# The feed-forward's transposed input: 32x32 blocks moved one by one, or through a scratch in DRAM

## The chip, the cores and the metric

The kernel runs on one core of one Trainium2 chip. Its engines are TensorE (PE, matrix products), VectorE (DVE), ScalarE (ACT), GpSimd (POOL) and SyncE (SP); SP here only issues DMA transfers, and all DMA transfers of this kernel are issued by SP, one after the other. The metric is the device time of one execution in microseconds (us). The kernel before takes 1178.18 us, the median of three runs from 1177.28 to 1179.29 us.

## The reference, cut to what matters

One transformer block on 2048 rows of 448 numbers, in float32: layer norm, attention with 16 query heads and one shared key and value head, a residual sum, then a second layer norm and a gated feed-forward with 1792 hidden features, and a second residual sum.

```python
x = A_x                                   # 1 x 2048 x 448
h = x + _A_ref(_layernorm(x), wq, wk, wv, wo)      # attention, head width 28
h2 = h + _B_ref(_layernorm(h), w1, w3, w2)

def _B_ref(x, w1, w3, w2):                # 448 -> 1792 -> 448
    gate = jnp.einsum("bsd,df->bsf", x, w1)
    up = jnp.einsum("bsd,df->bsf", x, w3)
    h = _silu(gate) * up
    return jnp.einsum("bsf,fd->bsd", h, w2)
```

The change concerns `_layernorm(h)`, the input of the feed-forward, on its way from rows to columns.

## The kernel before, in words

**Quarters and blocks.** The 2048 rows are worked in four quarters of 512 rows (`t` from 0 to 3, `T = 512`), and a quarter in four blocks of 128 rows (`n` from 0 to 3). The residual stream of a quarter stays in SBUF as `X[t]`, with rows on partitions. The matrix products need the normalized rows turned round, with the 448 features on partitions: the tile `xh`, which holds the features in three chunks of 128 partitions and a fourth of 64, and 512 columns, one for each row of the quarter.

**Order of the work.** The order on every engine is written out by hand. After a short start (projections of the queries, keys and values), the attention runs over 256 steps (16 per group of four heads, four groups a quarter), and between them hangs work from a table: `at(s, fn, ...)` puts a call at step `s`. The feed-forward follows: 14 steps `k` a quarter (`NF = 14`, 128 hidden features each), with a second table: `on(t, k, fn, ...)` puts a call behind step `k` of quarter `t`, and `k + 0.5` is a place a little later in the same step. In each step PE makes the two products of 128 hidden features (`ffn1_half`, two halves of the array working side by side, line 1025) and, for the step before, the product back to 448 (`ffn2_half`, line 1025 too). Between the halves stands `settle`, a 1x1 ACT copy out of the PSUM bank (line 1029): PE goes on to the other half only after it.

**The path of the feed-forward's input.** For each block, `ln_norm` (line 213) writes the normalized rows into a tile `xn`; `blocks` (line 225) transposes it on DVE in blocks of 32x32, so that inside every 32x32 block features and rows have changed places, while the blocks themselves still stand where they stood. Sixteen DMA transfers a block (`moves`, line 238), so 64 a quarter, then bring these small blocks to their places in `xh`, from SBUF to SBUF. Each takes 32 partitions of `xn`, and three or four pieces of 32 numbers (128 bytes) of each. `move(m)` issues the next `m` of the waiting transfers. Last, `split_x` (line 243 on ACT, 247 on DVE) divides `xh` chunk by chunk into a rounded part and a rest, the two operands of the products.

**When.** The input of quarter 0 is made during the attention (transposes behind groups of quarters 1 and 2, and two moves at each of 16 steps). The input of quarter `t` from 1 to 3 is made during the feed-forward of quarter `t - 1`: transposes behind steps 1, 3, 5 and 7, with all 16 moves at once, and `split_x` behind steps 9 to 12 (at `9.5 + n`). Quarter 1 differs: its transposes stand behind steps 1, 3, 4 and 6, the moves of its first two blocks follow at once, and the other 32 are spread, seven at each of the steps 4 to 8. In that quarter SP also has the last weights of the feed-forward to load, between the moves: `load_w13` (lines 175 to 177, six transfers a step) and `load_w2` (line 184), into buffers which the attention has left.

**Queues.** SP works its transfers off in program order, and a transfer whose data is not ready holds all that stand behind it. The transfers take eight semaphores in turn, and a transfer waits until the one eight places ahead of it has landed where it takes over that semaphore. ACT, DVE and PE work off their orders in the same way.

Of the kernel before, what the change touches and what calls it, by code (L numbers as in the profile page):

```python
# [8 lines left out]
F32 = mybir.dt.float32  # L9
# [7 lines left out]
P = 128  # L17
S = 2048
D = 448
# [3 lines left out]
T = 512  # L23
NT = S // T
NQ = T // P
# [10 lines left out]
def block_kernel(  # L36
# [13 lines left out]
    ve, se, ge, pe, sy = nc.vector, nc.scalar, nc.gpsimd, nc.tensor, nc.sync  # L50
# [4 lines left out]
    def f(ap):  # L55
        return ap.bitcast(F32)
# [6 lines left out]
    dr_pool = ctx.enter_context(tc.tile_pool(name="dr", bufs=2, space=DRAM))  # L63
# [152 lines left out]
    XT = {}  # L216

    def xt_tiles():
        return [xt_pool.tile([P, m, T], F32R, name=name) for m, name in ((4, "xh"), (3, "xl"))]

    XD, moves = {}, []

    def blocks(t, n):
        xt = ln_pool.tile([P, 512], F32, name="xn", bufs=4)
        ve.transpose(xt[:, :D], LN[t][3][n][:, :D])
        if n == 0:
            XT[t] = xt_tiles()
        to = f(XT[t][0])
        x4 = xt.rearrange("i (c b j) -> i c b j", c=4, b=4)
        for a in range(4):  # L230
            for b in range(4):
                m = 4 if b < 2 else 3
                moves.append((to[32 * b : 32 * b + 32, :m, n * P + 32 * a : n * P + 32 * a + 32],
                              x4[32 * a : 32 * a + 32, :m, b]))

    def move(m):
        for _ in range(min(m, len(moves))):
            sy.dma_start(*moves.pop(0))  # L238

    def split_x(t, *cs, high=None):  # L240
        raw, hi = XT[t][:2]
# [589 lines left out]
    def at(s, fn, *args):  # L831
        todo.setdefault(s, []).append((fn, args))
# [6 lines left out]
    for i in range(NI - 1):  # L839
        e = NC * (i + 1)  # L840
# [3 lines left out]
    for t in range(NT - 1):  # L844
        e = NC * NG * (t + 1)


        if t == 1:
            at(e + 14.7, ln_stats, 0, NQ - 1)
            at(e + 14.7, ln_rstd, 0)  # L850
        for n in range(NQ):
            at(e + 14.7, wo_rows, t, n)
            for m in {(1, 1): (0,), (1, 2): (1,), (2, 0): (2, 3)}.get((t, n), ()):
                at(e + 14.7, ln_norm, 0, m, True)
                at(e + 14.7, blocks, 0, m)
            if t == 0 and n == NQ - 1:
                continue
            late = NC * NG * (t + 2) + 14 if t < 2 else LAST - 12
            at(e + 14.7 if n < NQ - 1 else late + 0.7, ln_stats, t, n)
        if t:  # L860
            at(late + 2, ln_rstd, t)
            for k in range(16):
                at(e + 16 + k, move, 2)
    for c in range(4):
        at(LAST - 12 + 2 * c, lambda c: split_x(0, c, high=ve.tensor_copy), c)
    for t in range(NT - 1):
# [12 lines left out]
    for s in range(AHEAD, LAST):  # L879
        i, c = divmod(s, NC)  # L880
        n, kt = divmod(c, NQ)
# [221 lines left out]
    def on(t, k, fn, *args):  # L1103
        after.setdefault((t, k), []).append((fn, args))
# [20 lines left out]
    on(0, 12, ln_rstd, tl)  # L1125
    for t in range(1, NT):
        for n in range(NQ):
            k = (1, 3, 4, 6)[n] if t == 1 else 1 + 2 * n
            on(t - 1, k, ln_norm, t, n)
            on(t - 1, k, blocks, t, n)  # L1130
            if t > 1 or n < 2:
                on(t - 1, k, move, 16)
            on(t - 1, 9.5 + n, split_x, t, n)
    for k in range(4, 9):
        on(0, k, move, 7)

    prev = None
    for t in range(NT):
# [68 lines left out]
```

## Time and profile before

| what | value |
|---|---|
| median of three runs | 1178.18 us |
| the profiled execution | 1178.61 us |
| its span, first to last instruction | 1176.8 us |
| PE busy | 1150.6 us, 98% of the span |
| DVE busy | 806.6 us, 69% |
| ACT busy | 764.3 us, 65% |
| POOL busy | 328.9 us, 28% |
| mean granted clock of PE | 0.993 of full speed |
| attention ends, feed-forward begins | at about 739 us |

A row of the timeline gives the start, the duration, the engine, the line, the operation, what it writes and reads and, in square brackets, how long the engine stood idle before it and what ended that. A row with a count (x16) holds that many instructions, and its duration runs from the first one's start to the last one's end. SPq is SP's issuing of transfers; the duration is that of the issue, and the transfer itself lands later. A row of the windows view gives a stretch of the span, its length, and for PE, PE's weight loads, DVE, ACT and POOL the busy time in it with the number of instructions; then the granted clock, the share of the 16 DMA engines that was busy, and GB/s.

### The profile page before, as it was taken

To read this page: it belongs to the slowest core of one execution; us is meant where nothing else is said; L and a number is where in the kernel's file an instruction comes from. 1 tells how busy PE (TensorE), PEld (TensorE's weight loads), DVE (VectorE), ACT (ScalarE), POOL (GpSimd) and SP (SyncE) were. 2 spreads that over 40 slices of the span, in tenths; PEclk is the share of its full clock that TensorE was granted. 3 is DMA by queue.
4 is the path that set the end of the run, shared out by engine and by line. 5 is a ranking of instruction groups with operands and counts; after the bars stand their busy time and mean duration, and the time that the engine had idled before them with its cause. 6 is when DMAs were issued, how large, how long until landed. Compare 5 with 4: busy or idle time off the path is not lost.

```text
span 1176.8 us, 25851 instructions
## 1 busy us (share of the span) xinstructions
PE 1150.6 (98%) x10154; PEld 772.5 (66%) x10154; DVE 806.6 (69%) x1498; ACT 764.3 (65%) x1587; POOL 328.9 (28%) x242
## 2 busy tenths in 40 slices
PE   8999999999999999999999999999499999999998
PEld 6664444446444445444455443799499999999997
DVE  8878999997999988989988962544253454344333
ACT  5649999996999997999997999312122222222221
POOL 5312001111110111110111013334265555556552
PEclk9999999999999999999999999999799999999999
DMA  4010100001000001100011100223201101100000
GB/s 165 10 37 1 43 12 9 19 22 39 19 19 7 14 24 40 32 20 15 7 40 36 20 18 19 64 68 95 58 33 17 18 1 40 17 9 32 1 2 32
DMA packets 67834, 34.51 MB, mean 29 GB/s; under 512 B 44672, under 2 KB 62336, under 8 KB 67712
## 3 DMA queue, kind: packets, MB, share of 16 engines
q1 hardware_dynamic: 67712, 32.86, 10.6%
q8 instruction: 80, 1.31, 0.5%
q14 instruction: 42, 0.34, 0.1%
HBM read 20.37 MB, written 3.80 MB: 21 GB/s over the span
## 4 chain that ended last, share of the span: by engine, by line
PE 85%; SPq 7%; DVE 2%; ACT 2%; DMA 1%; issue 1%; POOL 0%; ACTq 0%; DVEq 0%; POOLq 0%
PE po L424 20%; PE pb L408 19%; PE pa L1025 16%; PE pa L324 10%; PE pb L1025 8%; PE pb L166 4%; SPq L238 4%; PE po L1025 4%; PE pa L166 3%; SPq L177 1%; SPq L175 1%; ACT OT L431 1%; SPq L176 1%; ACT ab L345 1%; DVE mx L334 1%
## 5 line engine op out<-in xcount | busy, mean ns | idle before, releaser
L334 DVE TENSOR_REDUCE mx<-pa 128x1 f32<-128x512 f32 x689 | 440.2, 685 | 22.2 <-PE pb L408 13.1
L408 PE MATMUL pb<-qs,KS 32*128 32x512 f32 x3072 | 384.8, 425 | 0.0
L415 ACT ACTIVATE pt<-pb 128x512 f32<-128x512 f32 x684 | 366.1, 621 | 20.0 <-PE pb L408 17.3
L408 PEld LDWEIGHTS pb<-qs,KS 32*128 32x128 f32 x3072 | 233.9, 182 | 132.8 <-ACT pt L415 66.9
L324 PE MATMUL pa<-KS,qs 32*128 32x512 f32 x886 | 311.6, 459 | 1.5 <-ACT ab L345 0.2
L1025 PE MATMUL pa<-xl,qs 64*128 64x512 f32 x1044 | 193.6, 389 | 0.0
L324 PEld LDWEIGHTS pa<-KS,qs 32*128 32x128 f32 x886 | 138.6, 182 | 83.2 <-DVE mx L334 46.4
L424 PE MATMUL po<-pt,VA 128*32 128x512 f32 x1368 | 182.2, 604 | 0.4 <-ACT pt L415 0.4
L1025 PE MATMUL pa<-xh,qs 64*128 64x512 f32 x739 | 157.6, 389 | 0.0
L455 POOL TENSOR_TENSOR OT<-OT,rb 128x512 f32<-128x512 f32 x15 | 19.5, 1300 | 458.2 <-DMA rb<-sd 206.9
L1025 PE MATMUL pb<-w2s,pt 64*128 64x448 f32 x1050 | 143.2, 360 | 0.0
L1025 PEld LDWEIGHTS pa<-xl,qs 64*128 64x128 f32 x1044 | 140.2, 185 | 3.2
L1035 DVE TENSOR_TENSOR pt<-pa,pt 128x512 f32<-128x512 f32 x49 | 33.9, 691 | 152.7 <-ACT pt L1033 146.6
L1025 PEld LDWEIGHTS pb<-w2s,pt 64*128 64x128 f32 x1050 | 123.1, 184 | 2.4 <-DVE pt L1041 0.4
L352 DVE CUSTOM_DVE_ANT_0 ab<-pa,ab 128x512 f32<-128x512 f32 x138 | 93.6, 686 | 39.0 <-PE pa L324 27.1
L1025 PEld LDWEIGHTS pa<-xh,qs 64*128 64x128 f32 x739 | 106.7, 185 | 3.1
L415 ACT ACTIVATE xl<-pb 128x512 f32<-128x512 f32 x170 | 99.7, 611 | 9.0 <-PE pb L408 6.8
L415 ACT ACTIVATE xh<-pb 128x512 f32<-128x512 f32 x170 | 104.5, 633 | 0.0
L1033 ACT ACTIVATE pt<-pa 128x512 f32<-128x512 f32 x49 | 29.3, 597 | 96.9 <-PE pa L1025 92.8
L424 PE MATMUL po<-xl,VA 128*32 128x512 f32 x340 | 89.4, 605 | 0.0
L424 PE MATMUL po<-xh,VA 128*32 128x512 f32 x340 | 89.4, 605 | 0.0
L345 ACT ACTIVATE ab<-pa 128x512 f32<-128x512 f32 x138 | 82.2, 608 | 6.5 <-PE pa L324 4.9
(156 smaller groups left out, 1412.9 us busy)
## 6 DMA issues: line engine op xcount, KB each, us to landing
rb<-sd SPq DMA_DIRECT2D x64, 64.0 KB
QR<-OT SPq DMA_DIRECT2D x60, 56.0 KB
QR<-in_B_w_dram SPq DMA_DIRECT2D x16, 192.0 KB
X<-in_A_x_dram SPq DMA_DIRECT2D x3, 896.0 KB
out_dram<-X SPq DMA_DIRECT2D x3, 896.0 KB
xh<-xn SPq DMA_DIRECT2D x128, 16.0 KB
xh<-xn SPq DMA_DIRECT2D x128, 12.0 KB
w<-in_B_w_dram SPq DMA_DIRECT2D x8, 192.0 KB
```

Source lines behind the costliest of these rows:

```text
L166: pe.matmul(ps, lhs[b][:, cb, lsl], (rhs[2] if ca == 3 and len(rhs) == 3 else rhs[a])[:, ca, rsl], start=(k == 0), stop=(k == len(terms) - 1),
L238: sy.dma_start(*moves.pop(0))
L324: pe.matmul(ps, QS[i][r, 0, n * P : (n + 1) * P], KS[0][r, kt * T : (kt + 1) * T] if keys is None else keys[r], start=True, stop=True)
L334: ve.tensor_reduce(self.to(), ps, axis=AX.X, op=ALU.max)
L345: se.activation(self.ab, ps, AF.Relu)
L352: ve.tensor_tensor_reduce(self.ab, ps, self.ab, 1.0, -3.0e38, ALU.add, ALU.max, self.to())
L408: pe.matmul(self.ps, KS[k % 2][r, c * P : (c + 1) * P], QS[i][r, k // 2], start=(k == 0), stop=(k == 2))
L415: se.activation(f(PT[i, c, p][:, jj]), self.ps, AF.Exp, bias=0.0, scale=SCALE)
L424: pe.matmul(PO[i][32 * j : 32 * j + 32], VA[:, c], f(PT[i, c, j // 2][:, j % 2]), start=(c == 0), stop=(c == NC - 1))
L1025: pe.matmul(ps[:, : rhs.shape[-1]], lhs, rhs, start=bool(first), stop=bool(last), skip_group_check=True)
L1033: se.activation(sg, ps[0], AF.Silu)
L1035: ve.tensor_tensor(sg, ps[1], sg, op=ALU.mult)
```

## The change

Quarter by quarter, the DVE transposes stay as they are. The 32x32 blocks no longer go straight to `xh`. A tile `xr` of 448 x 512 numbers in DRAM is laid out as the finished transpose; four transfers a block (line 231) write the blocks into it, each taking 32 partitions of `xn` and all 14 pieces of 128 bytes of each. When the four blocks of a quarter are written, `fetch` (lines 236 and 237) reads the scratch into `xh` with two transfers, in rows of 2 KB. So a quarter has 16 transfers out and two back. In quarter 1 the transposes move to the steps 1, 3, 5 and 7 of the other quarters, and `fetch` stands behind step 7 (at 7.5). For quarter 0 all four transfers of a block are issued with its transpose, and `fetch` comes during the attention, 18 steps into the last quarter.

```diff
-    XD, moves = {}, []
+    XD, XR = {}, {}
 
     def blocks(t, n):
         xt = ln_pool.tile([P, 512], F32, name="xn", bufs=4)
         ve.transpose(xt[:, :D], LN[t][3][n][:, :D])
         if n == 0:
-            XT[t] = xt_tiles()
+            XR[t] = dr_pool.tile([D, T], F32, name="xr")
+        to = XR[t].rearrange("(k i) (n a j) -> n a i k j", i=32, n=NQ, j=32)
+        x3 = xt[:, :D].rearrange("i (k j) -> i k j", j=32)
+        for a in range(4):
+            sy.dma_start(to[n, a], x3[32 * a : 32 * a + 32])
+
+    def fetch(t):
+        XT[t] = xt_tiles()
         to = f(XT[t][0])
-        x4 = xt.rearrange("i (c b j) -> i c b j", c=4, b=4)
-        for a in range(4):
-            for b in range(4):
-                m = 4 if b < 2 else 3
-                moves.append((to[32 * b : 32 * b + 32, :m, n * P + 32 * a : n * P + 32 * a + 32],
-                              x4[32 * a : 32 * a + 32, :m, b]))
-
-    def move(m):
-        for _ in range(min(m, len(moves))):
-            sy.dma_start(*moves.pop(0))
+        sy.dma_start(to[:, 0:3], XR[t][0:384].rearrange("(c p) e -> p c e", p=P))
+        sy.dma_start(to[0:64, 3], XR[t][384:448])
...
         if t:
             at(late + 2, ln_rstd, t)
-            for k in range(16):
-                at(e + 16 + k, move, 2)
+            if t == 2:
+                at(e + 18, fetch, 0)
...
     for t in range(1, NT):
         for n in range(NQ):
-            k = (1, 3, 4, 6)[n] if t == 1 else 1 + 2 * n
-            on(t - 1, k, ln_norm, t, n)
-            on(t - 1, k, blocks, t, n)
-            if t > 1 or n < 2:
-                on(t - 1, k, move, 16)
+            on(t - 1, 1 + 2 * n, ln_norm, t, n)
+            on(t - 1, 1 + 2 * n, blocks, t, n)
             on(t - 1, 9.5 + n, split_x, t, n)
-    for k in range(4, 9):
-        on(0, k, move, 7)
+        on(t - 1, 7.5, fetch, t)
```

The first place is SP's queue during the feed-forward of quarter 0, from the last weight loads to the store of the finished quarter (`out_dram<-X_77`). `xh` is the feed-forward's input, `xn` the transposed block, `w_wo` and `w_1` are weights. Before:

```order
L184 DMA w_wo_11638<-in_B_w_dram 128x448
L184 DMA w_wo_11640<-in_B_w_dram 128x448
L175 DMA w_1_11639<-in_B_w_dram 128x3x128
L176 DMA w_1_11639<-in_B_w_dram 64x128
L177 DMA w_1_11639<-in_B_w_dram 64x128
L175 DMA w_1_11639<-in_B_w_dram 128x3x128
L176 DMA w_1_11639<-in_B_w_dram 64x128
L177 DMA w_1_11639<-in_B_w_dram 64x128
L184 DMA w_wo_11640<-in_B_w_dram 128x448
L238 DMA xh<-xn 32x4x32 x2
L238 DMA xh<-xn 32x3x32 x2
L1098 DMA out_dram<-X_77 128x1792
```

In the changed kernel the same stretch, from the last block's four writes on, reads:

```order
L231 DMA xr<-xn 32x14x32 x4
L184 DMA w_wo_11557<-in_B_w_dram 128x448
L184 DMA w_wo_11559<-in_B_w_dram 128x448
L175 DMA w_1_11558<-in_B_w_dram 128x3x128
L176 DMA w_1_11558<-in_B_w_dram 64x128
L177 DMA w_1_11558<-in_B_w_dram 64x128
L175 DMA w_1_11558<-in_B_w_dram 128x3x128
L176 DMA w_1_11558<-in_B_w_dram 64x128
L177 DMA w_1_11558<-in_B_w_dram 64x128
L184 DMA w_wo_11559<-in_B_w_dram 128x448
L236 DMA xh<-xr 128x3x512
L237 DMA xh<-xr 64x512
```

The nine weight loads have kept their place; the last four of 64 moves behind them have become the two reads of the scratch, and the writes of the last block stand ahead of the loads.

The second place is DVE in the feed-forward of quarter 0, around the transpose of quarter 1's last block (`X_78` is quarter 1's residual stream; lines 1035 and 1041 belong to the hidden features of a step, 496 and 483 prepare weights; in the changed kernel those line numbers are lower by one). Before:

```order
L1035 TENSOR_TENSOR pt<-po,pt 128x512
L1041 TENSOR_TENSOR pt<-pt 128x512
L213 TENSOR_SCALAR xn<-X_78,mv,rs 128x448
L225 STREAM_TRANSPOSE xn<-xn 128x448
L496 CAST w2s<-w_ks 128x448
L483 CAST qs<-OT 128x1024
```

Now:

```order
L1034 TENSOR_TENSOR pt<-pa,pt 128x512
L1040 TENSOR_TENSOR pt<-pt 128x512
L213 TENSOR_SCALAR xn<-X_78,mv,rs 128x448
L225 STREAM_TRANSPOSE xn<-xn 128x448
L495 CAST w2s<-w_wo_11557 128x448
L482 CAST qs<-w_0_11556 128x1024
```

The pair of lines 213 and 225 has gone from step 6 to step 7; the pair of the third block went from step 4 to step 5 in the same way. Apart from these two pairs PE, DVE, ACT and POOL have the same instructions in the same order as before.

## The prediction

> **What bounds the kernel now.** I read the page's busy times first, then a table of windows to find where PE rests, then the timelines of PE, ACT and SP at that place.
>
> ```profile
> span 1176.8 us, 25851 instructions
> PE 1150.6 (98%) x10154; PEld 772.5 (66%) x10154; DVE 806.6 (69%) x1498; ACT 764.3 (65%) x1587; POOL 328.9 (28%) x242
> ```
> ```profile
> 490.00:510.00 20.00, 19.89 (x195) 9.18 (x192) 18.27 (x36) 19.73 (x41) 0.00 (x0) 1.00 0.06 10
> 660.00:675.00 15.00, 14.76 (x143) 6.59 (x142) 13.46 (x26) 14.66 (x30) 0.00 (x0) 1.00 0.07 11
> 815.00:825.00 10.00, 7.91 (x73) 7.33 (x69) 4.48 (x7) 1.45 (x4) 4.32 (x3) 1.00 0.38 100
> 825.00:840.00 15.00, 0.58 (x2) 0.50 (x4) 0.65 (x2) 0.84 (x3) 0.37 (x1) 0.52 0.38 103
> 840.00:900.00 60.00, 60.00 (x538) 57.52 (x536) 28.75 (x49) 15.84 (x46) 35.11 (x21) 0.98 0.07 21
> ```
>
> PE is the bound: it rests 1176.8 - 1150.6 = 26.2 us in all. 16.5 of these lie in one hole, 2.09 us in the window from 815 and 14.42 in the one from 825. In the attention, where quarter 0's moves go out (the windows from 490 and 660), the rest is 0.11 and 0.24 us, and from 840 on none. So the case is decided in the hole. PE and ACT around it:
>
> ```profile
> 821.36 1.55 PE L1025 MATMUL pb<-w2s,pt 64*128 64x448 f32 x12
> 839.42 0.79 PE L1025 MATMUL po<-xl,qs 64*128 64x512 f32 x1 [16.51 <-ACT pexp L1029]
> ```
> ```profile
> 819.87 0.14 ACT L1029 ACTIVATE pexp<-pb 1x1 f32<-1x1 f32 x1
> 838.68 0.63 ACT L243 ACTIVATE xl<-xh 128x512 fp32r<-128x512 f32 x1 [18.68 <-DMA xh<-xn]
> 839.22 0.14 ACT L1029 ACTIVATE pexp<-po 1x1 f32<-1x1 f32 x1
> ```
>
> Read backwards: PE waits for a settle (line 1029); the settle stands on ACT behind `split_x` (line 243); that waits 18.68 us for quarter 1's `xh`. The `xh` of step 9.5 is simply late, because of SP:
>
> ```profile
> 759.38 11.31 SPq L238 DMA_DIRECT2D xh<-xn  x16
> 778.06 10.83 SPq L238 DMA_DIRECT2D xh<-xn  x16
> ...
> 834.75 2.59 SPq L238 DMA_DIRECT2D xh<-xn  x4
> ```
> ```profile
> L238 SPq DMA_DIRECT2D xh<-xn x64: 585/599/1702, 759.4 to 836.7; - x64
> ```
>
> The 64 moves of quarter 1 and the weight loads between them keep SP issuing from 759.4 to 837.3 us. A move occupies SP for 0.60 us (0.64 with the gap), whatever it carries; 64 are 41 us of the 78. The last is issued at 836.74 and ACT goes on 1.94 us later.
>
> What the hole costs is more than the rest, since PE resumes at a lower granted clock (0.52 in the window from 825). DVE's line 1035 comes once a step:
>
> ```profile
> 811.37 0.69 DVE L1035 TENSOR_TENSOR pt<-pa,pt 128x512 f32<-128x512 f32 x1 [2.54 <-ACT pt L1033]
> 818.60 0.69 DVE L1035 TENSOR_TENSOR pt<-pa,pt 128x512 f32<-128x512 f32 x1
> 844.20 0.69 DVE L1035 TENSOR_TENSOR pt<-po,pt 128x512 f32<-128x512 f32 x1 [3.55 <-ACT pt L1033]
> ```
>
> A step is 818.60 - 811.37 = 7.23 us; the one with the hole takes 25.60. The loss is 18.37 us: 16.51 of rest and 1.86 of slow work.
>
> **When quarter 1's `xh` will be there.** All 18 transfers of a quarter are issues of SP; I take each as a move's, 0.64 us, since a weight load with three times a move's descriptors (line 175) takes no longer:
>
> ```profile
> 829.53 1.06 SPq L184 DMA_DIRECT2D w_wo<-in_B_w_dram  x2
> ...
> 832.31 0.59 SPq L175 DMA_DIRECT2D w<-in_B_w_dram  x1
> ...
> 834.12 0.58 SPq L184 DMA_DIRECT2D w_wo<-in_B_w_dram  x1
> ```
>
> SP issues 46 transfers fewer in quarter 1's stretch, 29 us, so it no longer runs behind. It now waits for the last transpose, at step 7:
>
> ```profile
> 805.53 0.69 DVE L1041 TENSOR_TENSOR pt<-pt 128x512 fp32r<-128x512 f32 x1 [0.70 <-ACT pt L1040]
> 925.17 0.69 DVE L1041 TENSOR_TENSOR pt<-pt 128x512 fp32r<-128x512 f32 x1 [0.70 <-ACT pexp L1029]
> 925.78 0.51 DVE L213 TENSOR_SCALAR xn<-X,mv,rs 128x448 f32<-128x448 f32 x1
> 926.32 0.65 DVE L225 STREAM_TRANSPOSE xn<-xn 128x448 f32<-128x448 f32 x1
> ```
>
> The second to fourth rows are quarter 2's last block behind the same step 7: the transpose ends 1.80 us after line 1041 begins. Quarter 1's line 1041 begins at 805.53, so the transpose ends at 807.33. Four issues bring SP to 809.95. Nine weight loads follow (829.53 to 834.75 above, 5.22 us): 815.2. There the read of the scratch is issued. Its nearest row is a load of 672 KB from DRAM onto 128 partitions, like the 768 KB here:
>
> ```profile
> 81.18 0.39 SPq L175 DMA_DIRECT2D OT<-in_A_wo_dram  x1
> ```
> ```profile
> 85.66 0.56 POOL L550 CAST WO<-OT 128x448 fp32r<-128x448 f32 x1 [7.10 <-DMA OT<-in_A_wo_dram]
> ```
>
> 4.48 us from issue to use, scaled by 768/672 at most 5.1 us; I take 4.8, as only part of it grows with the bytes. So `xh` lands at 820.0. ACT comes to `split_x` at 820.0 (behind its row at 819.87) and PE needs it later: it resumed 0.74 us after ACT's line 243 began, and undisturbed would have gone on at 839.42 - 16.85 = 822.57 (18.37 less some 1.5 lost after the restart). The deadline is 821.8, and 1.8 us are to spare: **nothing of the hole is left.** DVE's two moved pairs (1.2 us each) cost nothing: quarters 2 and 3 have them behind the same odd steps in a stretch in which PE never rests (window from 840). If that cover were gone they would cost 2.4 us, but as many leave steps 4 and 6.
>
> **The writes to DRAM** have no equal in the trace: pieces of 128 bytes, 448 a transfer. Of the last four transfers each DMA engine gets 4 x 448/16 = 112 pieces. The bounds for one:
>
> ```profile
> 883.00:941.00 58.00, 58.00 (x534) 56.51 (x533) 22.71 (x41) 13.31 (x41) 30.84 (x17) 1.00 0.11 18
> 546.80:550.30 3.50, 3.50 (x41) 1.47 (x36) 3.16 (x7) 3.41 (x8) 0.00 (x0) 1.00 0.05 7
> ```
> ```profile
> 546.90 0.35 SPq L446 DMA_DIRECT2D sd<-sm  x1
> 550.27 1.71 SPq L449 DMA_DIRECT2D rb<-sd  x4
> ...
> 675.17 0.37 SPq L446 DMA_DIRECT2D sd<-sm  x1
> 676.66 1.72 SPq L449 DMA_DIRECT2D rb<-sd  x4
> ```
>
> Below: from SBUF to SBUF, a quarter's 7168 pieces of 128 bytes take 0.11 x 58 x 16 = 102 us of engine time, 14 ns each. Above: the write `sd` to DRAM (128 pieces of 64 bytes, 8 an engine) is read again after 1.49 us at the quickest, 3.37 elsewhere; if all of 1.49 were those pieces, 186 ns each. In the window around `sd` the engines are busy 0.05 x 3.5 x 16 = 2.8 us for 128 pieces, 22 ns. I take 22: it is a write to DRAM in small pieces, the nearest row. Then 112 pieces need 2.5 us, no more than the four issues (2.6), and the last write lands 1.5 to 3.4 us behind its issue. In quarter 1 that is at most 812.8, under cover of the nine weight loads. In quarters 2 and 3 no load stands between, and the read waits for the writes: issues from 927.0 to 929.6, the last begun at 929.0, landed by 932.4, read issued, landed 4.8 us later: 937.2. PE's need there:
>
> ```profile
> 939.55 0.61 ACT L243 ACTIVATE xl<-xh 128x512 fp32r<-128x512 f32 x1
> ```
>
> By the same offset as in quarter 1 (1.8 us after ACT comes) the deadline is 941.4; 4.2 us to spare. Behind the waiting read stands only the store of the finished quarter, for which nobody waits. Quarter 0's read comes during the attention, some 80 us before its use; its removed moves can give back 0.35 us at most (the two windows above), counted as nothing.
>
> **The sum.** Profiled execution 1178.61 (1.81 around its span) - 18.37 + 0 = 1160.24. That execution stands 0.43 above the median, so 1159.8 against the median; I say **1160.0**.
>
> **The rivals.**
>
> A. *A rest of the hole stays* (chance 0.17). Only 1.8 us separate landing and deadline in quarter 1, and the read queues behind nine loads of 1.2 MB. For it: the 3.37 us rows show landings 1.9 us later than others of the same kind. Against: 46 fewer issues. At 70 ns a piece the writes end at 807.4 + 7.8 + 1.5 = 816.7; the loads, eight places behind, wait for them, and the read lands at 816.7 + 1.3 + 4.8 = 822.8: 1.0 us late, with restart some 1.5. With the 5.1 us read and a slow landing 3: 1161.5 to 1163.
>
> B. *The writes drain slowly in every quarter* (0.05, of which 0.03 end slower). At c ns a piece quarters 2 and 3 land at 927.0 + 112c + 1.5 + 4.8, quarter 1 at 807.4 + 112c + 1.5 + 1.3 + 4.8. The gain is eaten up when each is (18.37 - 3 x 1.86)/3 = 4.3 us late, near 110 ns; at 150 ns they are 8.7, 8.7 and 10.0 us late, with restarts 33 us, and the time is 1193. For it: a bound of 186 ns that the rows do not lower by themselves. Against: the 22 ns of the busy share. The Trainium skill ("DMA: Bandwidth & Descriptors", Specifications) speaks against the change here: it asks for 512 bytes or more for line rate, and has the DMA engine read, modify and write below that. It gives no price; were it a doubling of the 14 ns, the sum would stay as it is.
>
> C. *Another wait takes the hole's place* (0.02), say PE's next weights: DVE waits for a load in the hole's step too, but those loads now go out earlier; a wait of 2 us gives 1162.
>
> D. *The change doesn't do what it says* (0.01 within 0.2%): the wait at line 243 was not for `xh`, or SP is held ahead of the read by a load whose buffer is not free. The time stays 1178. Against: ACT moves 1.94 us after the last move's issue.
>
> **How the numbers follow.** The forecast has 0.75, its own range 1158.5 to 1161.5 (the three runs lie 2 us apart, the attention may give 0.35). Down to 1158.4 and up to 1164.0 takes in A and C and leaves out B and D. What a measurement of this kernel can tell from no change is 0.2%, 2.4 us. Faster: 0.75 + 0.17 + 0.02 and 0.01 of B, 0.95; same 0.02 (0.01 of B, and D); slower 0.03.
>
> **What would show it.** Right: PE's windows full from 800 us on; line 243's wait for the DMA gone or under 2 us; line 1035 every 7.23 us across step 9; SP idle before line 231 at step 7; ACT not waiting in quarters 2 and 3; SP's wait ahead of line 236 there of 2 to 4 us behind the last write's issue. Wrong: a wait of ACT on `xh<-xr` of several us in all three quarters (B), or in quarter 1 alone (A); busy share of the DMA engines above 0.2 in quarter 2's stretch.

## The result and the profile after

The changed kernel takes 1161.35 us (median of four runs, 1160.38 to 1162.24) against 1178.4 us for the kernel before (four runs, 1177.28 to 1179.29). The ratio is 0.9856, with a 95% interval from 0.9839 to 0.9873. The profiled execution took 1160.38 us. Lines behind the changed functions stand one lower than before: the settle is line 1028, the split 242, the hidden features 1034.

From the page of the changed kernel, the span, the busy times and the engines' shares in the chain that ended last:

```profile
span 1158.6 us, 25640 instructions
...
PE 1149.0 (99%) x10154; PEld 772.7 (67%) x10154; DVE 805.8 (70%) x1498; ACT 764.3 (66%) x1587; POOL 330.2 (29%) x242
...
PE 94%; ACT 2%; DVE 2%; issue 1%; DMA 1%; SPq 0%; POOL 0%; ACTq 0%; POOLq 0%
```

PE's work is the same; it is busy for 1149.0 us where it was 1150.6, and 1.6 us less fits the slow matmuls behind the hole. What went is above all its rest: 1158.6 - 1149.0 = 9.6 us, against 26.2. The windows (time, length, then busy time of PE, weight loads, DVE, ACT and POOL, the granted clock, the DMA share, GB/s) show where it went:

```profile
490.00:510.00 20.00, 19.89 (x196) 9.18 (x195) 18.26 (x36) 19.71 (x40) 0.00 (x0) 1.00 0.02 3
660.00:675.00 15.00, 14.92 (x146) 6.62 (x142) 13.72 (x26) 14.82 (x31) 0.00 (x0) 1.00 0.02 3
756.00:815.00 59.00, 59.00 (x454) 55.04 (x454) 29.71 (x47) 11.21 (x32) 27.11 (x16) 1.00 0.43 109
815.00:825.00 10.00, 10.00 (x95) 10.00 (x93) 4.82 (x8) 2.40 (x7) 5.99 (x4) 1.00 0.41 133
825.00:840.00 15.00, 15.00 (x142) 14.30 (x140) 9.15 (x14) 4.49 (x13) 8.32 (x5) 1.00 0.01 2
908.00:912.50 4.50, 4.50 (x44) 4.27 (x42) 1.55 (x4) 0.70 (x3) 3.37 (x2) 1.00 0.30 53
```

The two windows that held the hole, from 815 and from 825, are full and run at clock 1.00 (7.91 and 0.58 us of PE before, clock 0.52 in the second). The attention's windows gained 0.00 and 0.16 us. DVE's line 1034, once a step, now crosses step 9 at the steps' own pace:

```profile
811.48 0.69 DVE L1034 TENSOR_TENSOR pt<-pa,pt 128x512 f32<-128x512 f32 x1 [3.17 <-ACT pt L1032]
...
818.71 0.69 DVE L1034 TENSOR_TENSOR pt<-pa,pt 128x512 f32<-128x512 f32 x1 [3.47 <-ACT pt L1032]
...
825.94 0.69 DVE L1034 TENSOR_TENSOR pt<-po,pt 128x512 f32<-128x512 f32 x1 [1.92 <-ACT pt L1032]
```

Twice 7.23 us, where the step with the hole had 25.60. On SP's timeline for quarter 1 (start, length, line, how many issues) the reason stands:

```profile
803.46 0.60 SPq L177 DMA_DIRECT2D w<-in_B_w_dram  x1
807.47 1.91 SPq L231 DMA_DIRECT2D xr<-xn  x4
...
810.42 1.48 SPq L175 DMA_DIRECT2D w<-in_B_w_dram  x1
...
814.93 0.58 SPq L184 DMA_DIRECT2D w_wo<-in_B_w_dram  x1
815.55 0.43 SPq L236 DMA_DIRECT2D xh<-xr  x1
816.03 0.49 SPq L237 DMA_DIRECT2D xh<-xr  x1
```

SP is idle from 804.06 to 807.47: it waits for the last transpose, where before it was behind. The four writes, nine loads and the read follow, and ACT meets the data almost on time (its first row below; the last is the same place in the next quarter):

```profile
819.97 0.14 ACT L1028 ACTIVATE pexp<-pb 1x1 f32<-1x1 f32 x1
820.90 0.63 ACT L242 ACTIVATE xl<-xh 128x512 fp32r<-128x512 f32 x1 [0.79 <-DMA xh<-xr]
821.87 0.16 ACT L1028 ACTIVATE pexp<-po 1x1 f32<-1x1 f32 x1 [0.33 <-PE po L1024]
...
921.29 0.61 ACT L242 ACTIVATE xl<-xh 128x512 fp32r<-128x512 f32 x1
```

The wait for `xh` is 0.79 us instead of 18.68, and the settle behind it (line 1028) now waits for PE, so PE is not held up. In the next quarter there is no wait at all.

### The profile page after: what moved, and what is told of

Read it like the earlier page. It is cut to its first block, busy times and chain, and to the rows that moved or that the text cites. A ratio compares the mean times of both kernels' runs of the same rounds, so it can differ in the third digit from the quotient of the medians.

```text
span 1158.6 us, 25640 instructions
## 1 busy us (share of the span) xinstructions
PE 1149.0 (99%) x10154; PEld 772.7 (67%) x10154; DVE 805.8 (70%) x1498; ACT 764.3 (66%) x1587; POOL 330.2 (29%) x242
## 4 chain that ended last, share of the span: by engine, by line
PE 94%; ACT 2%; DVE 2%; issue 1%; DMA 1%; SPq 0%; POOL 0%; ACTq 0%; POOLq 0%
PE po L423 21%; PE pb L407 20%; PE pa L1024 18%; PE pa L323 10%; PE pb L1024 9%; PE pa L166 5%; PE pb L166 4%; PE po L1024 4%; PE pb L1070 1%; ACT OT L430 1%; ACT ab L344 1%; DVE mx L333 1%; PE pb L273 0%; ACT pt L414 0%; PE po L166 0%
```

## The experiments

The theory: SP's number of issues made the hole, quarter 1 alone carries the gain, and a cover of a microsecond or two is left behind its read. The rivals: the order of the transposes did it, the attention's 64 moves did it, or the way through DRAM costs something that the gain hides.

### Quarter 1 alone, and all but quarter 1

The first kernel uses the scratch for quarter 1 alone and the 64 moves for the others; the second does the opposite (`SCRATCH = (0, 2, 3)`), and keeps the old steps for quarter 1.

```diff
+    SCRATCH = (1,)
...
     def blocks(t, n):
...
+        if t not in SCRATCH:
...
+                    moves.append((to[32 * b : 32 * b + 32, :m, n * P + 32 * a : n * P + 32 * a + 32],
+                                  x4[32 * a : 32 * a + 32, :m, b]))
+            return
```

> Quarter 1 alone goes through the scratch; quarters 0, 2 and 3 keep their 64 moves each. Queue theory (the whole gain is SP's backlog of issues in quarter 1): 1160 to 1163 us, all of the gain, ACT's wait at split_x of quarter 1 under 1.5 us. Rival (the gain is spread: fewer issues and packets help the attention and the later quarters as well): 1164 to 1170.

> The other part alone: quarters 0, 2 and 3 go through the scratch, quarter 1 keeps its 64 moves and its steps 1, 3, 4 and 6. Queue theory: 1177 to 1179 us, no gain, with the hole of some 16.5 us after step 9 of quarter 0 still there. Rival (spread gain): 1172 to 1176.

Quarter 1 alone: 1161.07 us (1160.55 to 1163.45), ratio 0.9855 (0.9839 to 0.9871), the whole gain; ACT's wait at quarter 1's split is 0.35 us. All but quarter 1: 1179.89 us, ratio 1.0004 (0.9995 to 1.0014), none of it, and 0.9 us above the expected range. In the second kernel ACT's split and a window over the hole read:

```profile
839.12 0.63 ACT L260 ACTIVATE xl<-xh 128x512 fp32r<-128x512 f32 x1 [17.69 <-DMA xh<-xn]
```
```profile
800.00:845.00 45.00, 29.44 (x255) 28.11 (x254) 12.32 (x23) 6.24 (x19) 14.44 (x8) 0.81 0.34 88
```

The hole stands there as before (15.6 us of rest in 45). So taking 46 issues away in each of the other quarters, the attention's too, is worth nothing that can be measured.

### The order alone

The kernel before with the change's steps 1, 3, 5 and 7 for quarter 1, and still 64 moves, 16 with each block.

```diff
-            k = (1, 3, 4, 6)[n] if t == 1 else 1 + 2 * n
+            k = 1 + 2 * n
...
-            if t > 1 or n < 2:
-                on(t - 1, k, move, 16)
+            on(t - 1, k, move, 16)
...
-    for k in range(4, 9):
-        on(0, k, move, 7)
```

> The kernel before with the change's order alone: quarter 1's transposes behind steps 1, 3, 5 and 7 and each block's 16 moves at once, still from SBUF to SBUF, so still 64 issues. The last move then stands ahead of nine loads instead of behind them. Queue theory: SP still runs behind; the nine loads (5.2 us) and little more drop out from ahead of the last move, which is issued near 831 instead of 836.7, the hole shrinks by 6 us: 1171 to 1174 us. Rival (the order, not the number of issues, makes the gain): 1160 to 1163.

1174.12 us (1173.44 to 1175.18), ratio 0.996 (0.9945 to 0.9975): 4 to 5 of the 17 us, just above the expected 1171 to 1174. SP's last block of moves and ACT's wait:

```profile
823.10 10.30 SPq L238 DMA_DIRECT2D xh<-xn  x16
```
```profile
834.69 0.63 ACT L243 ACTIVATE xl<-xh 128x512 fp32r<-128x512 f32 x1 [11.95 <-DMA xh<-xn]
```

Quarter 1's last move is still issued at about 833, since 64 moves keep SP behind; ACT waits 11.95 us instead of 18.68, and PE rests 9.65 us there instead of 16.51. A new rest of PE of 1.07 us (at 824.49, for DVE) takes part of that back. The order is a small part by itself, and the number of issues the large one.

### The same bytes in 64 writes

Each write cut in four, the same pieces to the same places: 64 writes and two reads a quarter. Then the same cut for `t == 1` alone (quarter 1) and for `t == 0` alone (quarter 0).

```diff
-            sy.dma_start(to[n, a], x3[32 * a : 32 * a + 32])
+            for k0, k1 in ((0, 4), (4, 8), (8, 11), (11, 14)):
+                sy.dma_start(to[n, a][:, k0:k1], x3[32 * a : 32 * a + 32, k0:k1])
```

> The changed kernel with each write to the scratch cut into four (4, 4, 3 and 3 of the 14 pieces a partition): the same path, bytes and pieces, but 64 writes and 2 reads a quarter. Queue theory: 48 issues more in quarter 1 at 0.5 to 0.64 us put the read back to 825 to 832 and bring a hole of 8 to 16 us back there; in quarters 2 and 3 the last block's 16 issues (8 to 10 us) leave the read 1 to 4 us late. Together 1172 to 1188. Rival (the way through DRAM and its two reads make the gain, not the number of issues): 1160 to 1163.

1192.60 us (1190.86 to 1193.4), ratio 1.0114 (1.0099 to 1.0129): 31 us behind the changed kernel, and slower than the kernel before. That is beyond what I expected, since I had looked for the cost at the reads of quarters 1 to 3 and not in the attention. By the start of the feed-forward, which the four sums' transfers in front of it mark (`sm<-OT` at 760.72 instead of 740.00), 20.7 us are lost already in the attention; quarter 1 lost some 11 more. In quarters 2 and 3, where a loss was expected too, ACT waited 1.37 and 1.14 us at its split, and PE did not rest. The two halves apart:

> The changed kernel with each write cut in four in quarter 1 alone (64 writes and two reads there, 16 and two in the others). Issue theory: SP is held in the feed-forward of quarter 0 as in the run that cut all of them, which lost 11.8 us there: 1171 to 1173.5 us. Rival (that loss came from what the attention had delayed): 1160 to 1163 us.

> The changed kernel with each write cut in four in quarter 0 alone, whose writes lie in the attention. Issue theory: SP issues the transfers of the softmax sums 11 us late at two places, DVE's reciprocals and TensorE wait for them: 20 to 21 us lost, 1180 to 1182.5 us. Rival (the attention is not bound by SP, and the loss there was of another cause): 1160 to 1163 us.

Cut in quarter 1 alone: 1170.41 us (1169.95 to 1173.8), ratio 0.9933 (0.9911 to 0.9955). Cut in quarter 0 alone: 1182.08 us (1180.13 to 1184.78, ten runs), ratio 1.0025 (1.0014 to 1.0037). Against the changed kernel 9.1 and 20.7 us; together 29.8 of the 31.3. The first is just under its expected 1171, and 1.5 us of the whole stay unassigned; the second is as expected. For the cut in quarter 1, SP, ACT and PE:

```profile
811.56 7.64 SPq L232 DMA_DIRECT2D xr<-xn  x16
...
824.29 0.43 SPq L237 DMA_DIRECT2D xh<-xr  x1
```
```profile
829.32 0.63 ACT L243 ACTIVATE xl<-xh 128x512 fp32r<-128x512 f32 x1 [9.66 <-DMA xh<-xr]
```
```profile
830.05 0.79 PE L1025 MATMUL po<-xl,qs 64*128 64x512 f32 x1 [7.52 <-ACT pexp L1029]
```

The read is issued 8.74 us later than in the changed kernel (815.55), and the hole is back with 7.52 us. For the cut in quarter 0, SP's timeline in the attention shows 32 writes and, behind six loads, the transfers of the softmax sums. The same two rows of the changed kernel stand behind it, then DVE and PE of the cut kernel.

```profile
456.65 16.34 SPq L232 DMA_DIRECT2D xr<-xn  x32
...
476.56 2.47 SPq L438 DMA_DIRECT2D sm<-OT  x4
```
```profile
454.31 4.09 SPq L231 DMA_DIRECT2D xr<-xn  x8
...
462.56 2.47 SPq L437 DMA_DIRECT2D sm<-OT  x4
```
```profile
480.35 0.25 DVE L445 RECIPROCAL sm<-sm 128x16 f32<-128x16 f32 x1 [10.11 <-DMA sm<-OT]
```
```profile
481.24 0.79 PE L324 MATMUL pa<-KD,qs 32*128 32x512 f32 x1 [8.73 <-DVE mx L352]
```

The sums leave SP 19.91 us after the first write instead of 8.25, so 11.7 us later. DVE comes to its reciprocal and stands 10.11 us; the maxima that PE needs are queued behind it, and PE rests 8.73 us. The same happens at 633 (32 writes of 16.06 us; PE rests 6.26). So issues on SP are not free in the attention. The 64 moves before cost nothing there, and SP's rows of the kernel before show where they stood:

```profile
452.89 0.59 SPq L177 DMA_DIRECT2D QR<-in_B_w_dram  x1
462.26 2.47 SPq L438 DMA_DIRECT2D sm<-OT  x4
464.83 2.61 SPq L238 DMA_DIRECT2D xh<-xn  x4
```

They came behind these sums, four to twelve in a row, and ahead of the sums SP had stood idle for 8.8 us. The changed kernel gives eight writes ahead of the six loads and the sums, and from the end of the last load (461.91) to the sums SP has 0.65 us left (at the second place 2.97). Whether the place or the number in a row decides was not tested apart.

### The read later

To find the cover: more transfers on SP ahead of quarter 1's read. The first try sent them from `pexp`.

```diff
     def fetch(t):
+        if t == 1:
+            dummy = dr_pool.tile([8 * P, 32], F32, name="dummy", bufs=1)
+            for k in range(8):
+                sy.dma_start(dummy[k * P : (k + 1) * P], pexp)
         XT[t] = xt_tiles()
```

> The changed kernel with eight small transfers (16 KB from SBUF to a scratch in DRAM that nobody reads) ahead of quarter 1's read of the scratch, about 5 us of SP's time. Deadline theory (ACT waited 0.79 us in the changed kernel, PE's deadline is 1.0 us behind that): the read lands 4 to 5 us later, PE rests 3 to 4 us and loses up to 1.9 more to a lower clock: 1164.5 to 1167.5 us. Rival (PE has more cover than that in this step): 1160 to 1163.

1174.45 us (1173.67 to 1176.32), 7 us beyond the expected range. This run measures something else: the settle writes `pexp`, so ACT had to wait until the added transfers had read it:

```profile
822.79 0.16 ACT L1032 ACTIVATE pexp<-pa 1x1 f32<-1x1 f32 x1 [14.01 <-DMA dummy<-pexp]
```

An experiment that adds a transfer must take its source from a tile that nobody writes. With a constant instead, eight of them and then four:

```diff
-                sy.dma_start(dummy[k * P : (k + 1) * P], pexp)
+                sy.dma_start(dummy[k * P : (k + 1) * P], ident[:, :32])
```

> The changed kernel with eight more transfers of 128x32 numbers, from a constant that nobody writes, on SP just ahead of quarter 1's read (about 3.7 us of issue). Deadline theory: the read lands 3.7 us later, near 824.55, where TensorE needs ACT's split from 821.8 on; it loses 2.75 us and 1.5 to 1.9 us of slow clock behind the pause: 1164.5 to 1166 us. Rival (there is more cover behind the read than the rows show): 1160 to 1161.5 us.

> As the run with eight, with four transfers (about 1.85 us). Deadline theory: the read lands near 822.7, 0.9 us behind the deadline, and up to 1.5 us of slow clock: 1161 to 1163 us. Rival (more cover): 1160 to 1161 us.

Eight: 1163.95 us (1162.87 to 1164.79), ratio 0.9869 (0.9854 to 0.9884). Four: 1160.9 us (1160.43 to 1163.32), ratio 0.9848 (0.9831 to 0.9864). For the eight, SP, ACT, PE and a window:

```profile
815.13 3.75 SPq L238 DMA_DIRECT2D dummy<-ident  x8
818.92 0.43 SPq L240 DMA_DIRECT2D xh<-xr  x1
```
```profile
824.03 0.63 ACT L246 ACTIVATE xl<-xh 128x512 fp32r<-128x512 f32 x1 [4.27 <-DMA xh<-xr]
```
```profile
824.76 0.75 PE L1028 MATMUL po<-xl,qs 64*128 64x512 f32 x1 [2.14 <-ACT pexp L1032]
...
828.28 0.39 PE L1028 MATMUL po<-xl,qs 64*128 64x512 f32 x1
```
```profile
823.00:830.00 7.00, 5.24 (x34) 4.40 (x36) 1.72 (x3) 1.44 (x4) 2.37 (x1) 0.76 0.05 12
```

For the four, ACT and DVE's row of each step:

```profile
819.52 0.14 ACT L1032 ACTIVATE pexp<-pb 1x1 f32<-1x1 f32 x1
821.88 0.63 ACT L246 ACTIVATE xl<-xh 128x512 fp32r<-128x512 f32 x1 [2.22 <-DMA xh<-xr]
```
```profile
818.25 0.69 DVE L1038 TENSOR_TENSOR pt<-pa,pt 128x512 f32<-128x512 f32 x1 [3.47 <-ACT pt L1036]
...
825.84 0.69 DVE L1038 TENSOR_TENSOR pt<-po,pt 128x512 f32<-128x512 f32 x1 [1.99 <-ACT pt L1036]
```

With four the time can't tell the theories apart: 1160.9 us lies in the rival's range and just below the expected 1161 to 1163. The profiled execution can: the step takes 825.84 - 818.25 = 7.59 us, 0.36 more than 7.23. ACT's split began at 821.88, so 821.52 would have been in time, 1.86 us after ACT came to it (819.66). That measures the deadline, in one execution: the prediction had 1.8. It fits the 64 writes, where ACT's waits of 1.37 and 1.14 us cost PE nothing. In the changed kernel ACT comes at 820.11, the deadline is 821.97 and the split begins at 820.90: 1.07 us are left. With eight the same DVE row comes 11.22 us after the one before (818.35 to 829.57), a loss of 3.99: 2.14 of rest and 1.85 of slow work. The time is 3.5 us above the changed kernel's repeat below, half a microsecond less than the expected range.

### The read earlier, and the way through DRAM taken out

Three kernels ask whether anything of the transport is still on the path: `fetch` ahead of the nine loads; one write of the residual rows as they lie and the two reads, in place of sixteen writes (its feed-forward works on other numbers, neither normalised nor transposed; DVE's work stays); and the changed kernel once more beside them.

```diff
-        on(t - 1, 7.5, fetch, t)
+        on(t - 1, 7, fetch, t)
```
```diff
...
-        for a in range(4):
-            sy.dma_start(to[n, a], x3[32 * a : 32 * a + 32])
+        if n == NQ - 1:
+            flat = XR[t].rearrange("d e -> (d e)").rearrange("(p q) -> p q", p=P)
+            sy.dma_start(flat, X[t].rearrange("p n d -> p (n d)"))
```

> The changed kernel with the read of the scratch ahead of the last nine weight loads (behind step 7 instead of 7.5). Deadline theory: SP waits 2 to 3 us for the last write, issues the read near 812, it lands near 817, ACT's wait is gone; PE had no hole in the profiled run, so 1160 to 1161.5 us, and if the runs of the changed kernel above 1161 come from a landing just past the deadline, these are gone. Rival (the loads, now 3 us later, are late): 1163 to 1170.

> The transport cut to one write (the residual rows as they lie, in long rows, instead of 16 writes of transposed blocks) and two reads a quarter; so the feed-forward works on other numbers. DVE's norm and transposes stay. Theory (the 18 transfers are fully hidden): 1159.5 to 1161.5 us, as the changed kernel. Rival (small pieces, or SP's issues, still cost PE something in the attention or the later quarters): 1156 to 1159.

> The changed kernel again, beside the run with the early read. Both theories: 1160 to 1162.5 us; the spread of its runs against that of the early read tells whether its landing sometimes misses the deadline.

They took 1160.42 us (1160.02 to 1161.59; ratio 0.9843, 0.9829 to 0.9858), 1160.70 (1160.27 to 1161.29; 0.9846, 0.9829 to 0.9862) and 1160.47 (1159.94 to 1161.38; 0.9843, 0.9828 to 0.9858): the same. In the first, SP and ACT:

```profile
807.50 1.91 SPq L231 DMA_DIRECT2D xr<-xn  x4
812.43 0.38 SPq L236 DMA_DIRECT2D xh<-xr  x1
```
```profile
820.06 0.62 ACT L242 ACTIVATE xl<-xh 128x512 fp32r<-128x512 f32 x1
```

SP stands 3.0 us (809.41 to 812.43) until the last write has landed, ACT no longer waits, and the time does not move, since 0.79 us of waiting lay under the deadline anyway. The kernel that makes one plain write shows no cost of the sixteen writes in pieces of 128 bytes. The changed kernel's own two sets of runs lie 0.9 us apart, so nothing below a microsecond is read out of these medians. The runs with the early read spread over 1.6 us and the changed kernel's over 1.4, so a landing past the deadline is not what makes its slower runs.

## Why the prediction was right, and where its terms were off

**The hole and its cause: right.** 18.37 us were to go; the spans differ by 1176.8 - 1158.6 = 18.2 us. The medians differ by 17.05 us, and by 18.5 when the changed kernel was run again (1178.97 - 1160.47), so that 1161.35 against the forecast 1160.0 lies within what the runs themselves differ by. Quarter 1 alone brings it, all but quarter 1 brings nothing, and quarter 1's writes cut in four bring 7.52 us of the rest back with the same bytes at the same places.

**When SP is done: right to 0.35 us, by luck.** Two errors cancel. The four writes took 1.91 us, 0.48 each, not 0.64: a move's issue was too dear a row for them. The nine loads took 6.1 us and not 5.22, since one of them held SP for 1.48 us where 0.43 is usual (at 810.42 above); why is open. So the read was issued at 815.55 (815.2 forecast).

**The read: a little short.** 4.8 us were taken, between 4.48 and 5.1. From its issue to ACT's split the changed kernel shows 5.35 us and its second profile 5.11. Other runs in which ACT waited for the read show 4.64 (quarter 1 alone through the scratch), 4.79 (four added transfers), 5.11 (eight) and 5.03 (the cut in quarter 1): 5.0 in the mean, and up to 0.25 over the prediction's upper bound. In the changed kernel `xh` was therefore there at 820.9 instead of 820.0.

**The deadline: right, on a loose term.** 1.8 us after ACT comes was forecast; the run with four added transfers gives 1.86. The forecast took 1.5 us off for slow work after the restart, where its own rows had 1.86; with these it would have said 2.2. The spare time is 1.07 us (1.1 in the second profile, 1.5 with quarter 1 alone), not 1.8. Rival A, the rest of the hole, was nearer than 1.8 suggested: it needs SP a microsecond or two later, and the run with eight shows it, at 1163.95 us. The prediction's A put 1.5 us of restart on top of the lateness; the run with eight lost 3.99 us for about 2.4 of lateness (824.03 against 819.76 + 1.86), 1.6 on top.

**The DRAM pieces: overestimated, without effect.** One window holds the last four writes of quarter 2 alone (908 in the windows above): 0.30 x 4.5 x 16 / 1792 = 12 ns a piece, where 22 was taken and the lower bound was 14. The row of `sd` was not a wrong neighbour but was misread: of the 2.8 us in its window the DMA view gives 2.3% of 16 engines, 1.3 us, to one 16 KB packet of an instruction queue. The 2.9% of the transfers themselves, 1.6 us, make 13 ns a piece. By the Trainium skill ("DMA: Bandwidth & Descriptors", Specifications) pieces below 512 bytes make the engine read, modify and write; no such price shows at 128 bytes here. Rival B's slow drain isn't there either: the DMA engines' share in quarter 2's stretch (864 to 922) is 0.15, under the 0.2 that was to speak for B. In quarter 2 SP's rows are

```profile
908.74 1.87 SPq L231 DMA_DIRECT2D xr<-xn  x4
912.59 0.38 SPq L236 DMA_DIRECT2D xh<-xr  x1
```

so SP waits 1.98 us behind the last issue, and 1.6 in quarter 3: at or just under the forecast 2 to 4. ACT does not wait in either.

**The attention: right in sum, thin in reasoning.** The prediction counted the removed moves as nothing and left it there. Its windows gained 0.16 us. But it did not ask what eight issues at one place would delay, and the run with 32 at each of those places shows that SP can hold up the softmax sums: at the first place 0.65 us of spare time stood between them and a delay.

**DVE's moved pairs: right.** They lie at steps 5 and 7, before 815, and PE is busy for all of the window from 756 to 815, as in the kernel before.

## What to carry to other kernels

When a queue's engine is the late one, count issues, not bytes: 64 small transfers took SP 41 us in a stretch in which 18 with the same content leave it 3.4 us idle before the last block. Here the gain came only from the one place where the data was late; the same saving elsewhere was worth nothing, while adding issues at two places with little slack cost 20 us. Before moving transfers to another place in a queue, look for what stands behind them there and how much slack it has.

## What the runs showed of the hardware that was not expected

- SP's issue does not grow with the pieces. A write of 32 partitions with 14 pieces took 0.48 us, the same write with 3 or 4 pieces also 0.48 (7.64 us for 16), a move from SBUF to SBUF with 3 or 4 pieces 0.60. Why the move is dearer is open.
- 128-byte pieces to DRAM took 12 ns of a DMA engine, no more than the 14 ns from SBUF to SBUF. From the end of the last write's issue to the read that depends on it SP stood 1.6 and 2.0 us in quarters 3 and 2, and 3.0 us in quarter 1 of the run with the early read; why that is longer is open.
- A pause of 2.14 us on PE was followed by 3.5 us of slow matmuls (824.76 to 828.28, granted clock 0.76 in the window from 823) and cost 1.85 us on top; the pause of 7.52 us (the cut in quarter 1) cost 2.36 on top (17.11 - 7.23 - 7.52) and that of 16.51 us before 1.86, so the price does not follow the pause's length. A pause of some 0.1 us (the run with four added transfers) left the clock at 1.00. The Trainium skill ("TensorE: Matmul & The Clock Gate", Part 1) has the clock fall after an idle window of about 3.4 us and return after as long a busy one; the second agrees with the 3.5 us (after the pause of 7.52 us the slow matmuls lasted over 4), the first is longer than the pause that sufficed here.
